# First segment's first Q, K and V products in full fp32 from the weights as loaded, in an attention and MLP kernel

## The chip, the core and the metric

The kernel runs on one core of a Trainium2 chip. The core has five engines that work from queues of their own and wait for one another by semaphores: TensorE (PE: matmuls, and PEld for its weight loads), VectorE (DVE), ScalarE (ACT), GpSimd (POOL) and SyncE (SP, which here only issues DMAs). Each engine takes its instructions strictly in the order in which the program issues them. The metric is the device time of one execution in microseconds (us).

## The reference

Two branches share a layer norm of `x` (2048 tokens, 512 features). Their outputs and `x` are added.

```python
xn = layernorm(x)
out = x + A(xn) + B(xn)

# A: 32 heads of 16, the tokens in 4 segments of 512
q, k, v = xn @ wq, xn @ wk, xn @ wv            # per head
for s in range(4):
    logits = q_s @ k_s.T / 4 + mask            # -1e9 where query < key
    a_dot = softmax(logits) @ v_s
    a_mem = (phi(q_s) @ M) / (phi(q_s) @ z + 1e-6)
    o_s = g * a_mem + (1 - g) * a_dot          # g = sigmoid(beta), per head
    M += phi(k_s).T @ v_s ;  z += sum(phi(k_s))
A = concat(o_s) @ wo                            # phi(t) = t + 1 if t > 0 else exp(t)
# B: MLP with 1792 hidden features
B = gelu(layernorm(xn) @ w1 + b1) @ w2 + b2
```

## The kernel before, in words

**Numbers in two halves.** Inputs are fp32. For most products the kernel splits a number into a high and a low fp16 part and computes three fp16 products (high-high, high-low, low-high), summed in PSUM (`split3`, L463). A product with 512 input features has 4 blocks of 128, and so 12 matmuls. Weights are scaled by a power of two ahead of the split, taken from the mean square of the weights. `w_square` (L286) sums the squares on ACT, `w_scale` and `qk_scale` (L336, L324) bring the sums over all partitions by a small matmul and compute the scales on DVE, and `w_split` (L366) splits one piece. A piece marked "V" in `SPLIT` is split by ACT (high part) and DVE (low part) out of the raw weights. One marked "G" is scaled in place by POOL, rounded by ACT and subtracted by POOL. The raw weights lie in the same tiles in which the halves are put, two pieces further on, or in staging tiles borrowed from `pt`, `oT` and others.

**Tokens.** The first four token tiles are loaded, normalised (`ln`, L432), transposed by PE and split into `xnT` (`ln_out`, `ln_tr`, L447 to L459: ACT writes the high half, DVE the low one, both from PSUM).

**Units.** A unit is one segment and eight of the 32 heads: 16 units, of which units 0 to 3 are the first segment. `qk_proj` (L477) computes Q or K of a unit for 512 tokens. ACT and DVE split the result into `hl`, of which there is a single buffer, and SP stores it to DRAM three times and loads it back as stacks `qst` or `kst`. For K (and for Q after the first segment) `phi` is computed too, and `pk_nat` (L502) transposes it. `v_nat` (L558) computes V of 128 tokens. `m_jobs` (L583) computes the logits and takes the masked maximum of each row on DVE (L601). `s_jobs` (L622) computes them again, transposed, and ACT takes the exponentials. `pv` (L657) multiplies with V in fp32, `o_norm` (L681) normalises, `out_jobs` (L779) applies `wo`. The MLP is in pieces as well: `d_jobs` (L717) is the hidden layer, `gelu` and `h_split` follow, and `e_part` (L758) is the second layer.

**The order of the work** is written out by hand as a string, `ORDER`: each letter names a stream (`streams`, L57), and the next job of that stream is issued. `BANKS` gives for each PSUM tile, in the order in which they are asked for, which of the eight banks it takes. Fourteen jobs of eight matmuls on constants (`warm_up`, L796) are strewn in.

Around the start the old order runs: loads of the tokens, of Q and K weights of the first head group ("qk"), of the other three ("QK"), of V; their squares on ACT among the norm and the transposes; the scales; then K of unit 0 (job 51 of 1307), the first V split, Q of unit 0 (67), the first hidden-layer product (68), K and Q of unit 1 (84, 99), and V of the four token blocks (88, 115, 118, 123). The first row maxima are jobs 92 to 95.

Of the kernel before, what the change touches and what calls it, by code (L numbers as in the profile page):

```python
# [19 lines left out]
P = 128  # L20
# [24 lines left out]
SPLIT = {"qk": "VV", "QK": "GVGVGV", "v": "VVVV", "1a": "GVGVGVG", "2a": "GVGVGVG", "1b": "GVGVGVG", "2b": "GVGVGVG",  # L45
# [11 lines left out]
def streams():  # L57
# [31 lines left out]
    for m in PARTS:  # L89
# [3 lines left out]
        if m == "v":  # L93
# [3 lines left out]
    zero = [("zero", 0), ("const",), ("zero", 1)]  # L97
    return [norm, again, wts, [("par2",)], zero, keys, queries, nat, maxi, soft, vals_p, heads, memo, vals, hid, act,
            mlp, outs, accs, [("warm", n) for n in range(14)]] + split
# [3 lines left out]
    "aacttcucccecuttauttvvvvaceaaccvueataccvctatbvwcwtcdfwvtuxxxhtyxxyxxgoyxswtxocwvxwyowfcxynoyziiiiyvzgoyiozczyozy"  # L103
    "pziiniznipiAnaciqizAzpooiimvBivhooAAiiqiqvpjpqjqqijqijziqiqwcjqqjiAsmzkBzkkkqjAiojssiqAjjoioBAjjaAfApooBgskkpkk"
    "jpjqlohoopjjljoojiiqilApkkkkjiqqiqAijqqjijqjjgpiiakkkkifpplqiiqqqqqqslooioppoiiioloosijiaaqaBsjqqjiqjijqiqjqiii"
    "paqkkmkkqiqajqqqjqjaaihbojjjgpBmkkkkBfoopjjloojjqljlooijqiBkpkkkijqipqiqjqqjiiqjjqqijqqiqmipikkkkmlignhillfpnrr"
    "mjjrjqjjnaiijpnsiiikkkkijoiijopojiqjiqijsrjikkkmkihlspomfoljjqqjqjmjgloojmkkmkkjqqjjqaqqjqjiqqjiqkkkmkippliiohf"
    "ooapliqqiqmqipgoopqqqiiiqqiqlsmoopoioppqiioojiqijqjqijooijjsoapamkkkkamjisithpqjisqjqjqaqjjaqqiiqqikkkkpiaalblo"
    "sfojqjqjqjqqjmjglkkmkmkjjoojjjomhojiipkkkkaiiipnplnpiliifnimigniilriarrmmsijjrjijoajqiiqjqiskkkksijqjqiqjqijqjq"
    "iqjiqipikkkkoilmhfoqpljjqjqmjgpjjpoooolmkmkkkohijsiqjqpiqijqiqjqqijiqqiqqiqjiqiipkkkkmoipllfmqqgoooopopopsjqjqj"  # L110
    "qjqqjqiiqpqiqiqipooqjiqiiqpilsmoooooaapikkskkpiqjaqjaaqjqqqqjijqjqaiamskkmkkblfoljmjhgjqqjqjqjqlomkkkkmjjjmooij"
    "iojiojiipkkkkpiifiinpiliinlnimlgmrjjjspnrojiqiqjqiqijqipkkkkqijqjsirjqijqjqijqiqiispkkkmkrpillfompgooopmjqjjooj"
    "mjqojsqiilkkkkpiqijqiqjqiqijjqijqiqjiqipsikkkkoilpolfojmjgpqjqjqqjjookkklmkpoiqjiqjqiqijqijopjjqiqiiqiqiqqipskk"
    "ppikoikplspoooqjqjljqqjqjjooolkpkpkkqqjqspmqqjjqqqqjqpqqjqqjmkkkkpmqqqlqqlqqqqlqqqrrrr"
# [5 lines left out]
    "012345670123546137402651372405614372051643720516437205164307265143027653027653062753062706532750362570376205376"  # L120
    "205376205362705326705326705326710452376104526371045263045320645036245063245063245063245063712450637124506372145"
    "061435601453601345601345601354607132547601325476013254670123546703456374056743065704365074356074630574630574630"
    "745630745630475162304753016247530164275031765420316750136017563017605310576310576035173650713650713657013657420"
    "136507421365021365021365021365021365021365210356210764235107462351074654213607326107326107326107326107613027613"
    "052743061527413056274153062741530627410532764105237641052376410523170562413760254103215043250143025143502145032"
    "145032145034215034276031524371605243716502654302643560423560423560423560423560427160427160427160427160427160427"
    "106427103564271035642710642710267410267410627410741674216704231560742031576402316574021365740213657402136574012"
    "365741230657412360531260523610523610352601365021635021635021635021635021632501637245016245062140562415061254065"
    "124065124065124065124056140256317405263174263172467321734621763241763241763417623417620345120342510342510342571"
    "60257"  # L130
# [17 lines left out]
def infini_mixer_kernel(ctx: ExitStack, tc: tile.TileContext, x, wq, wk, wv, wo, beta, w1, b1, w2, b2, out):  # L148
# [64 lines left out]
    qksc = cst.tile([P, 4, 2, NG], F32, name="qksc")  # L213
# [110 lines left out]
    def qk_scale(g0, n):  # L324
# [7 lines left out]
        V.tensor_scalar(qksc[:, 3, :, g0:g0 + n], s, float(2 ** 10), None, op0=OP.mult)  # L332
        V.tensor_tensor(qkcs[:, 0, g0:g0 + n], c[:, 0], c[:, 1], op=OP.mult)
        V.scalar_tensor_tensor(qkcs[:, 1, g0:g0 + n], f[:, 0], float(2 ** -16), f[:, 1], op0=OP.mult, op1=OP.mult)

    def w_scale(m):  # L336
# [18 lines left out]
        if m == "o":  # L355
# [27 lines left out]
    F1, S1, F2, S2, CG, SHH, C2, B1F = range(5, 21, 2)  # L383

# [76 lines left out]
    xnT = {}  # L461

# [14 lines left out]
    def qk_proj(i, which):  # L477
# [3 lines left out]
        split3(p, ((w, lambda w, k, a: w[:, g, a, P * k:P * k + P]),  # L481
                   (xnT[s], lambda t, k, a: t[:, k, a, :])), KT, True, True)
        phi = not (s == 0, s == NSEG - 1)[which]
        hl = sb.tile([P, 2, 512], F16, name="hl")
        A.activation(hl[:, 0, :], p, AF.Copy, scale=float(2 ** -16))
        if phi:
            e = sb.tile([P, 512], F32, name=("phq", "phk")[which])
            A.activation(e, p, AF.Exp, scale=qkcol(2, 1 - which, g))
# [8 lines left out]
        if phi:  # L497
            V.tensor_scalar(e, e, 1.0, qkcol(3, 1 - which, g), op0=OP.min, op1=OP.mult)
            V.scalar_tensor_tensor(e, p, 0.0, e, op0=OP.max, op1=OP.add)  # L499
            pqt[i, which] = e  # L500
# [383 lines left out]
```

## Time and profile before

| | |
|---|---|
| three runs, us | 708.18, 705.11, 708.0 (median 708.0) |
| profiled execution, us | 706.76 |
| its span, first to last instruction, us | 705.1 |
| granted TensorE clock over the span | 0.995 |
| instructions | 16658 |
| matmul records and their busy us | 6213, 683.4 |

The profile is one execution. Busy times are those of instructions at work on an engine; a PE that is busy is not at its peak for that, since the ends of its pipelined matmuls are modelled. A row of a group gives line, engine, operation, output and inputs, shape and count, then busy us and mean ns of one, then the engine's idle time just before them and what ended it. A row of the timeline gives the start, the busy time, and the instruction; several in a row of one kind are merged (x12). A row of the waits gives who waited for whom, the total, the times and the longest.

### The profile page before, as it was taken

The numbers are of one execution on the slowest core, as the hardware profiler recorded it, in microseconds if no ns is written. First come the engines' busy times: TensorE is split into PE (matmuls) and PEld (weight loads), VectorE is DVE, ScalarE is ACT, GpSimd is POOL, SyncE is SP. The second block draws the span as 40 slices with busy tenths as digits, with TensorE's granted clock in tenths as the row PEclk, the third lists the DMA queues.
The fourth block names the chain that finished last, engine by engine and source line by source line (L and its number), as shares of the span: only waits on it lengthen the run. The fifth ranks groups of instructions, "written<-read, shape, count | busy, mean of one in ns | idle before, by whom it ended". The sixth has DMA issues, their size and how long they took to land.

```text
span 705.1 us, 16658 instructions
## 1 busy us (share of the span) xinstructions
PE 683.4 (97%) x6213; PEld 395.6 (56%) x6213; DVE 545.1 (77%) x1734; ACT 517.8 (73%) x954; POOL 350.2 (50%) x532
## 2 busy tenths in 40 slices
PE   7779999999999999999999999999999999999997
PEld 6445656465644555567554456666554446555643
DVE  5599988798696867998689877969679676968533
ACT  6878888949786669568974597756686677887870
POOL 4265676463742435545454326355453445456652
PEclk9999999999999999999999999999999999999999
DMA  9966123141302322132222313141131313230001
GB/s 280 268 159 206 48 41 98 49 104 18 92 2 70 113 73 66 46 77 62 59 80 68 93 25 106 18 121 32 33 92 46 94 30 93 61 92 16 19 17 60
DMA packets 51791, 55.11 MB, mean 78 GB/s; under 512 B 4783, under 2 KB 40637, under 8 KB 51709
## 3 DMA queue, kind: packets, MB, share of 16 engines
q1 hardware_dynamic: 49404, 49.84, 25.0%
q0 software_dynamic: 2304, 4.20, 3.7%
q8 instruction: 49, 0.80, 0.5%
q14 instruction: 34, 0.27, 0.1%
HBM read 36.99 MB, written 17.04 MB: 77 GB/s over the span
## 4 chain that ended last, share of the span: by engine, by line
PE 74%; DVE 12%; ACT 8%; issue 2%; POOL 2%; DMA 1%; SPq 0%; POOLq 0%; DVEq 0%; ACTq 0%
PE ps L469 32%; PE ps L769 14%; PE ps L663 8%; PE ps L788 6%; PE ps L634 5%; PE ps L594 4%; DVE ps L601 4%; ACT pt L639 3%; PE ps L542 1%; ACT hT L736 1%; DVE mc L601 1%; DVE hT L729 1%; DMA pt<-in_A_wq_dram 1%; ACT hT L744 1%; PE ps L455 1%
## 5 line engine op out<-in xcount | busy, mean ns | idle before, releaser
L601 DVE CUSTOM_DVE_ANT_0 ps<-ps,mask 128x512 f32<-128x512 f32 (+3 forms) x512 | 234.1, 523 | 11.3 <-PE ps L594 10.0
L639 ACT ACTIVATE pt<-ps,qkcs 128x512 f32<-128x512 f32 (+1 forms) x384 | 205.4, 624 | 30.4 <-PE ps L634 25.5
L769 PE MATMUL ps<-w2s,hT 64*128 64x512 f16 x1344 | 175.9, 375 | 0.6 <-DVE fence L772 0.6
L469 PE MATMUL ps<-xnT,w1s 128*128 128x256 f16 x1344 | 159.0, 274 | 2.2 <-POOL w1s L378 0.8
L469 PEld LDWEIGHTS <-w1s 128*128 128x128 f16 x1344 | 129.1, 98 | 31.7 <-issue 11.5
L648 POOL TENSOR_SCALAR_AFFINE_SELECT pt<-pt 128x256 f32<-128x256 f32 x256 | 100.7, 422 | 80.8 <-ACT pt L639 80.1
L745 POOL TENSOR_TENSOR hT<-hh,hT 128x512 f16<-128x512 f32 x64 | 67.9, 1060 | 84.4 <-ACT hT L744 84.4
L769 PEld LDWEIGHTS <-hT 64*128 64x128 f16 x1344 | 74.3, 94 | 55.3 <-issue 8.1
L663 PE MATMUL ps<-pt,vt 128*32 128x256 f32 (+3 forms) x1024 | 77.7, 435 | 0.0
L601 DVE DVE_READ_ACCUMULATOR2_ANT mc<- 128x1 f32 x512 | 71.3, 139 | 0.1
L594 PE MATMUL ps<-kst,qst 48*128 48x512 f16 (+3 forms) x512 | 67.7, 297 | 1.9 <-DVE mc L601 0.7
L634 PE MATMUL ps<-qst,kst 50*128 50x512 f16 (+3 forms) x512 | 68.5, 297 | 1.0 <-DVE phk L499 0.6
L744 ACT ACTIVATE hT<-hh 128x512 f16<-128x512 f32 x64 | 36.7, 573 | 42.9 <-POOL hh L743 42.7
L729 DVE SCALAR_TENSOR_TENSOR hT<-ps,sc,sr 128x256 f32<-128x256 f32 x112 | 51.2, 477 | 21.7 <-PE ps L469 21.2
L663 PEld LDWEIGHTS ps<-pt,vt 128*32 128x32 f32 x1024 | 31.6, 109 | 40.9 <-issue 30.8
L743 POOL TENSOR_SCALAR hh<-hT,sc 128x512 f32<-128x512 f32 x64 | 42.2, 660 | 18.7 <-ACT hT L736 16.9
L736 ACT ACTIVATE hT<-hT,b1t 128x256 f32<-128x256 f32 x112 | 46.6, 496 | 4.0 <-DVE hT L729 3.8
L693 POOL TENSOR_TENSOR nN<-nN,oT 128x512 f32<-128x512 f32 x16 | 20.2, 1266 | 56.4 <-DVE oT L517 56.4
L469 PE MATMUL ps<-wvs,xnT 128*128 128x512 f16 x192 | 44.5, 382 | 3.6 <-DVE wvs L374 3.6
L634 PEld LDWEIGHTS <-kst 50*128 50x128 f16 x512 | 27.9, 94 | 30.6 <-issue 12.5
L469 PE MATMUL ps<-xnT,wqs 128*128 128x512 f16 x192 | 44.3, 380 | 0.6 <-DVE mc L601 0.6
L594 PEld LDWEIGHTS <-qst 48*128 48x128 f16 x512 | 28.2, 94 | 29.6 <-issue 13.3
(220 smaller groups left out, 931.7 us busy)
## 6 DMA issues: line engine op xcount, KB each, us to landing
kd<-hl SPq DMA_DIRECT2D x48, 128.0 KB
kst<-kd SPq DMA_DIRECT2D x32, 192.0 KB
qd<-hl SPq DMA_DIRECT2D x48, 128.0 KB
qst<-qd SPq DMA_DIRECT2D x32, 192.0 KB
acc<-in_A_x_dram SPq DMA_DIRECT2D x16, 256.0 KB
acc<-in_B_b_dram POOLq DMA_DIRECT2D x16, 256.0 KB, 4.2
out_dram<-acc SPq DMA_DIRECT2D x16, 256.0 KB
xt<-in_A_x_dram SPq DMA_DIRECT2D x14, 256.0 KB
```

What stands on the lines that cost most here:

```text
L469: T.matmul(p, wsl(ws, k, a), xsl(xs, k, b), start=s0 and i == 0, stop=s1 and i == 3 * n - 1)
L594: T.matmul(p[:, o:o + n], stk[i, 0][r, t, P * qb:P * qb + P], stk[i, 1][r, t, :n], start=True, stop=True)
L601: V.tensor_tensor_reduce(p[:, o:o + n], p[:, o:o + n], mask[:, 512 - n:], 1.0, -3e38, OP.add, OP.max, mc[i][:, 4 * b + t, qb:qb + 1])
L634: T.matmul(p[:, o:o + n], stk[i, 1][r, t, P * kb:P * kb + P], stk[i, 0][r, t, P * kb:], start=True, stop=True)
L639: A.activation(e[:, OFF[kbs[0]]:OFF[kbs[0]] + o], p[:, :o], AF.Exp, scale=qkcs[:, 1, i % NG:i % NG + 1])
L648: G.affine_select(v, v, pattern=[[0, 2], [1, P]], compare_op=OP.is_ge, fill=0.0, base=0, channel_multiplier=-1)
L663: T.matmul(p[32 * c:32 * c + 32, P * kb:], vt[s, kb][:, 4 * g + c, 16 * odd:16 * odd + 32], pt[i, 2 * c + odd][:, OFF[kb]:OFF[kb] + LEN[kb ...
L729: V.scalar_tensor_tensor(hz[:, fi, :], p[:, :256], col(CG + fh), srow[hs][:, own], op0=OP.mult, op1=OP.mult)
L736: A.activation(z, z, AF.Gelu_apprx_tanh, bias=b1t[:, FH * (j % 2) + f:FH * (j % 2) + f + 1])
L744: A.activation(hT[:, z, 0, :], t, AF.Copy)
L745: G.tensor_tensor(hT[:, z, 1, :], t, hT[:, z, 0, :], op=OP.subtract)
L769: T.matmul(pes[j][a], hTs[fh][r, fi, u, P * a:P * a + P], w2s[r, fo, v, :], start=n == 0 and m == 0, stop=fi == FH - 1 and m == 2, skip_gr ...
```

## The change

For the first segment Q and K of units 0 and 1 and V of all four token blocks are computed in full fp32 from raw weights and fp32 tokens: four matmuls of 512 columns in place of twelve in fp16. For that `first_tr` builds four fp32 tiles, each with the 512 tokens of 128 features (transposed by PE, copied out of PSUM by ACT or DVE in turns, in tiles borrowed from `oT`, `rt` and `phq`). `first_split` makes the fp16 halves of `xnT` for the first segment out of them, now from SBUF. The scales that the split path has in its weights are applied when results leave PSUM. The second piece of K is split by ACT and DVE instead of POOL, so that the raw weights of both second pieces last. All other products, of the first segment too, stay as they were, and so all weights are still split.

```diff
-SPLIT = {"qk": "VV", "QK": "GVGVGV", ...
+SPLIT = {"qk": "VV", "QK": "VVGVGV", ...
...
+    first = [("Xs", k) for k in range(KT)]
...
-    qksc = cst.tile([P, 4, 2, NG], F32, name="qksc")
+    qksc = cst.tile([P, 5, 2, NG], F32, name="qksc")
...
+        V.tensor_scalar(qksc[:, 4, :, g0:g0 + n], s, float(2 ** -6), None, op0=OP.mult)
...
-        if m == "o":
+        if m == "v":
+            V.tensor_scalar(col(SV0), col(SV), float(2 ** -6), None, op0=OP.mult)
+        elif m == "o":
...
+        if n == 0:
+            return first_tr(2 * b + k)
...
+    def first_tr(k):
+        p = dense()
+        for j in range(4):
+            T.transpose(p[:, P * j:P * j + P], lt[0, j // 2][j % 2][:, P * k:P * k + P], ident)
+        if k < 2:
+            t = sb.tile([P, 2, 512], F16, name="oT", bufs=4).rearrange("p a c -> p (a c)").bitcast(F32)
+        else:
+            t = sb.tile([P, 512], F32, name=("rt", "phq")[k - 2])
+        if k % 2:
+            V.tensor_copy(t, p)
+        else:
+            A.activation(t, p, AF.Copy)
+        x32[k] = t
+
+    def first_split(k):
+        h = xnT[0][:, k, 0, :]
+        A.activation(h, x32[k], AF.Copy, scale=1024.0)
+        V.scalar_tensor_tensor(xnT[0][:, k, 1, :], x32[k], 1024.0, h, op0=OP.mult, op1=OP.subtract)
...
+        raw = i < 2
+        if raw:
+            r = piece("qk"[which], g)
+            for k in range(KT):
+                T.matmul(p, r[:, P * k:P * k + P], x32[k], start=k == 0, stop=k == KT - 1)
+        else:
+            split3(...)
...
+        f = qkcol(4, 1 - which, g) if raw else float(2 ** -16)
+        A.activation(hl[:, 0, :], p, AF.Copy, scale=f)
...
-        A.activation(pkn[i], p.rearrange("p (a b) -> p a b", a=4), AF.Copy)
+        A.activation(pkn[i], p.rearrange("p (a b) -> p a b", a=4), AF.Copy, scale=qkcol(3, 0, i) if i < 2 else 1.0)
...
+        if s == 0:
+            for k in range(KT):
+                T.matmul(p, x32[k][:, P * b:P * b + P], piece("v", k), start=k == 0, stop=k == KT - 1)
+        else:
+            split3(...)
...
-                     scale=float(2 ** -16))
+                     scale=col(SV0) if s == 0 else float(2 ** -16))
```

`ORDER` and `BANKS` are new from the first letters to the last (1311 jobs, of which four are `first_split`, and as many PSUM tiles as before). The start of the new order: the two norm applications and all eight squares of Q and K weights come ahead of the four `first_tr` jobs (28, 30 to 32). Then, among others, the first x split (35), both V squares (37, 38), the scales of "QK" (40), the second x split (41), Q of unit 0 (45), the other x splits (47, 48), the "qk" splits (49, 50), two w1 squares (53, 54), K of unit 0 (55), V of blocks 0 and 1 (59, 60), Q of unit 1 (73), V of block 2 (74), the first two hidden-layer products (75, 78), the first row maxima (81, 82), K of unit 1 (86) and V of block 3 (94). The loads keep their sequence, except that those of w2 (second part of the first half) and of w1's second half are issued after the stores of Q of unit 0, and later K of unit 0, which stand on the same SP queue. From about job 200 on the same jobs have been issued in both orders, but for the four x splits and a handful of weight jobs: two splits of w2 and the squares of `wo` come later in the new one.

More of the change, by code (lines that the diff above doesn't have):

```diff
@@ L97, in streams @@
     zero = [("zero", 0), ("const",), ("zero", 1)]
+    first = [("Xs", k) for k in range(KT)]
     return [norm, again, wts, [("par2",)], zero, keys, queries, nat, maxi, soft, vals_p, heads, memo, vals, hid, act,
-            mlp, outs, accs, [("warm", n) for n in range(14)]] + split
+            mlp, outs, accs, [("warm", n) for n in range(14)]] + split + [first]
 ORDER = (
-    "aacttcucccecuttauttvvvvaceaaccvueataccvctatbvwcwtcdfwvtuxxxhtyxxyxxgoyxswtxocwvxwyowfcxynoyziiiiyvzgoyiozczyozy"
-    "pziiniznipiAnaciqizAzpooiimvBivhooAAiiqiqvpjpqjqqijqijziqiqwcjqqjiAsmzkBzkkkqjAiojssiqAjjoioBAjjaAfApooBgskkpkk"
@@ L105 @@
[L105 to L109, printed above, removed]
@@ L131 @@
+    "562370562370562370253625706325710463527014635216341562341653241563215632156321546315247630147630147630147630154"
+    "27015"
 )
```

58 lines of the change are left out of this document (32 added, 26 removed).

## The prediction

> **What bounds the kernel now.** I read the page's busy shares first, then the table of stretches, then the chain of waits at the start, and then the timeline of the first 60 us. The profiled execution took 706.8 us for a span of 705.1; 1.7 us lie around the span. The median of the runs shown is 708.0, so my sum, made against 706.8, stands 1.2 us under that median. About 0.5% (3.5 us: below 703.2 or above 710.3) is what a measurement of this kernel can tell from no change.
>
> ```profile
> PE 683.4 (97%) x6213; PEld 395.6 (56%) x6213; DVE 545.1 (77%) x1734; ACT 517.8 (73%) x954; POOL 350.2 (50%) x532
> ```
>
> The columns of the stretches are: bounds, length, busy us (count) of PE, PEld, DVE, ACT, POOL, the granted clock, DMA share, GB/s.
>
> ```profile
> 0.00:20.00 20.00, 15.87 (x113) 11.89 (x114) 12.29 (x47) 13.59 (x31) 9.30 (x23) 1.00 1.02 281
> 20.00:40.00 20.00, 15.63 (x100) 10.54 (x99) 12.81 (x48) 16.13 (x26) 8.02 (x9) 0.91 0.81 240
> 40.00:60.00 20.00, 15.94 (x100) 9.00 (x99) 18.95 (x46) 14.69 (x27) 11.81 (x11) 0.91 0.65 184
> 60.00:80.00 20.00, 19.08 (x164) 10.78 (x163) 19.62 (x79) 16.56 (x32) 12.39 (x13) 1.00 0.45 136
> 80.00:100.00 20.00, 18.76 (x219) 12.38 (x215) 18.21 (x73) 17.56 (x36) 14.43 (x24) 1.00 0.21 34
> 100.00:690.00 590.00, 586.98 (x5476) 336.45 (x5476) 458.82 (x1442) 438.60 (x805) 291.97 (x454) 1.00 0.24 62
> ```
>
> There are two kernels in one. From 100 us on PE is busy for 587.0 of 590 us. Before that PE is not the bound: it is idle for 14.7 of 100 us, and most of the warm-up matmuls (16.3 us in all, a row further down) are filler too. From 40 to 95 us the full engine is DVE (18.95, 19.62 and 18.21 of 20), with row maxima, weight splits and scalings. In the first 40 us nobody is full, and DVE loses time that it lacks later. So the early stage is DVE's load up to about 95 us plus what DVE waits before that, and from there on the end is a fixed amount of PE work away. DVE's waits in the first 100 us (total, times, longest):
>
> ```profile
> DVE w1s L374 <- ACT w1s L373: 2.9, 1, 2.9
> DVE st L395 <- DMA xt<-in_A_x_dram: 2.5, 1, 2.5
> DVE hT L729 <- PE ps L469: 2.4, 3, 1.0
> DVE hl L489 <- ACT phk L488: 1.7, 1, 1.7
> DVE nw L404 <- ACT nw L403: 1.6, 1, 1.6
> DVE fa L347 <- PE ps L345: 1.4, 1, 1.4
> DVE xnT L459 <- ACT xnT L458: 1.2, 1, 1.2
> DVE wks L284 <- PEq L870: 0.9, 1, 0.9
> DVE wks L374 <- ACT wks L373: 0.5, 1, 0.5
> DVE hl L489 <- ACT hl L485: 0.2, 1, 0.2
> ```
>
> They come to 15.3 us. The change can win only here: through fewer waits, through less DVE work ahead of 95 us, or by leaving PE less to do from there.
>
> **The products themselves.** Eight products change: Q and K of units 0 and 1, and V of the four token blocks. Each has 12 fp16 matmuls of 512 columns now and gets four fp32 ones.
>
> ```profile
> L663 PE MATMUL ps<-pt,vt 128*32 128x512 f32 x256 | 34.9, 603 | 0.0
> L594 PE MATMUL ps<-kst,qst 48*128 48x512 f16 x128 | 27.7, 378 | 0.2
> ...
> L594 PE MATMUL ps<-kst,qst 48*128 48x128 f16 x128 | 16.8, 214 | 0.0
> L801 PE MATMUL ps<-ones 128*128 128x256 f16 x112 | 16.3, 303 | 1.6 <-POOL ones L171 1.6
> ...
> L663 PE MATMUL ps<-pt,vt 128*32 128x128 f32 x256 | 13.8, 273 | 0.0
> ```
>
> Mean times hold a fixed latency that a stream hides, so I take slopes. An fp16 record costs (378 - 214) / 384 = 0.427 ns per column. An fp32 record costs (603 - 273) / 384 = 0.859 ns, and one fp32 matmul leaves two records: L663 issues 512 of them (16 units, 2 halves, 4 blocks, 4 tiles) and the four forms hold 1024 records. A product now streams for 12 x 512 x 0.427 = 2.62 us, and in fp32 for 8 x 512 x 0.859 = 3.52 us: +0.90 us each, **+7.2 us of PE work**. I cost it at nothing, since all eight lie ahead of 95 us, where PE has 14.7 us idle and most of 16.3 us of filler. Without that cover it costs 7.2 us less the earlier start below.
>
> **The start.** K of unit 0 starts at 18.30 now, because it needs split tiles of x and split weights.
>
> ```profile
> 13.51 0.57 ACT L458 ACTIVATE xnT<-ps 128x512 f16<-128x512 f32 x1
> 13.98 0.62 ACT L310 ACTIVATE wks<-pt 128x512 bf16<-128x512 f32 x1
> ...
> 17.73 1.06 ACT L310 ACTIVATE wvs<-wvs 128x1024 bf16<-128x1024 f32 x1
> ...
> 18.30 2.76 PE L469 MATMUL ps<-xnT,wks 128*128 128x512 f16 x12
> ...
> 20.86 7.34 SPq L276 DMA_DIRECT2D w1s<-in_B_w_dram  x4
> ...
> 23.77 1.70 ACT L310 ACTIVATE w1s<-w1s 128x1792 bf16<-128x1792 f32 x1 [0.37 <-DMA w1s<-in_B_w_dram]
> ...
> 50.11 0.69 DVE L601 CUSTOM_DVE_ANT_0 ps<-ps,mask 128x512 f32<-128x512 f32 x1
> ```
>
> Afterwards Q of unit 0 comes first and needs four fp32 tiles. The new order puts all eight squares of the Q and K weights ahead of ACT's first copy, where six stand now, so that copy moves from 13.51 to about 13.5 + 2 x 0.62 = 14.8. Two ACT copies of about 0.57 follow, and the first product starts at about 16.0, **2.3 us earlier** than 18.30.
>
> On SP's queue three stores and two loads of Q of unit 0 now pass in front of the second load of w2 (2a) and of all loads of w1's second half. These loads hold SP for 7.34 us from 20.86, with the first stores of K behind them. Moving the stores ahead costs nothing as long as the loads are in by about 33 us (w2) and 48 us (w1), where their squares stand in ACT's new queue. The squares of w1's first half still cannot start before 23.77: those loads keep their place.
>
> **DVE's waits after the change**, from the new order and these rows. The first 0.9 and 2.5 stay: 3.4. The wait in the normalisation (1.6) loses one square of 0.62 that stood ahead of its two activations: 1.0. The two waits at the transposed tiles and the first split (1.7) become about 2.2: ACT's copies are 1.3 later, and DVE's own two copies fill part of it. The two at hl (1.9) stay near 2.0, with other causes: the split of the second x tile and the hl of Q stand behind both V squares (1.06 each), and K's hl stands behind two w1 squares that start at 23.77 with 1.70 each. The wait of the V scale for PE (1.4) goes: its squares are done early. The split of w1 (2.9) becomes about 2.4, for the hl of Q of unit 1, which stands behind a w2 square of like length. Of the three at L729 one goes (1.0), which came from V waiting for its split weights: 1.4. The sum is 3.4 + 1.0 + 2.2 + 2.0 + 0 + 2.4 + 1.4 = 12.4, against 15.3: **-2.9 us**.
>
> **DVE's work ahead of 95 us.** Two of the four transposes are now copied by DVE before they are split.
>
> ```profile
> L729 DVE SCALAR_TENSOR_TENSOR hT<-ps,sc,sr 128x256 f32<-128x256 f32 x14 | 6.5, 474 | 2.4 <-PE ps L469 2.4
> ...
> L459 DVE SCALAR_TENSOR_TENSOR xnT<-ps,xnT 128x512 f16<-128x512 f32 x4 | 2.7, 687 | 1.3 <-ACT xnT L458 1.2
> ```
>
> The trace has no such copy; 0.47 (L729, half the length) and 0.69 (L459, the full length and one input more) bound it, and I take 0.6, nearer to the row of its length: 1.2 in all. One split of K goes from POOL to DVE.
>
> ```profile
> L374 DVE SCALAR_TENSOR_TENSOR w1s<-w1s,sc x5: 751/1460/1639, 34.0 to 72.2; 128x512 f16<-128x512 f32 x5
> ```
>
> That is 0.75 at the least and 1.64 at the most. I take 0.75, since this split comes near 20 us, when POOL has little to do. The three added scale columns are tiny instructions, 0.5 with their gaps. Together **+2.45 us**. The other way goes one DVE split of w2, which the new order puts behind the point that PE reaches at 95 us: **-0.75**. The split of x reads the same amount as now, and ACT's two copies (0.57 each) lie in the queue counted above. Two weight splits that used POOL's in-place scaling must now keep the raw weights, which is the same edit. The end of the order differs in where the last head's two steps stand between e parts; PE's queue there is the same, so I cost it at nothing. The rest of the order and the banks are new, too; a stretch with 587 of 590 us busy leaves them little to win, and perhaps 2 us to lose or win by chance.
>
> **The sum:** -2.9 + 2.45 - 0.75 = -1.2, so 706.8 - 1.2 = **705.6 us**: no change that can be told.
>
> **Rivals.**
>
> *Faster: DVE is fed early.* If ACT gets through its squares in time and V's splits, no longer urgent, meet a quiet POOL, the waits of 2.2, 2.0 and 2.4 shrink. All of them gone gives 705.6 - 6.6 = 699.0; half gives 702.3, which is this rival's time. For it: DVE's first row maximum comes at 50.11 although K and Q of unit 0 are done well before, so there is room. Against it: ACT was already busy 16.13 of 20 us from 20 to 40 us, and it gets two copies more.
>
> *Slower: PE becomes the early bound.* Six fp32 products (21.1 us) stand ahead of the first hidden-layer product in PE's queue, which can't come before 16.0 + 21.1 = 37 us. If the GELU, the e parts and DVE's row maxima then wait on PE, the 7.2 us are paid in full less the 2.3 of the earlier start: 706.8 + 4.9 = 711.7. It decides as soon as PE has no idle time or filler left between 37 and 95 us. Against it: PE idles 6.2 us between 40 and 100 by the stretches above, and V's products were only moved from there, not added.
>
> *Slower within the band: the two-input splits collide with POOL.* The split of x reads PSUM and SBUF now; afterwards it reads two SBUF tiles, like L374, whose row runs from 0.75 to 1.64 for one shape. If all four go from 0.69 to 1.46, that row's median, they cost 3.1 us: 708.7. Against it: POOL has little to do near 20 us. The Trainium skill states the rule for this, in "GPSIMD Engine Reference", Specifications: GpSimd's SBUF interfaces are shared with VectorE, with contention for VectorE instructions that have two SBUF inputs. By that rule this case would need POOL to be busy during the splits; the spread of L374 in this trace agrees with it.
>
> **How the numbers follow.** The forecast has 0.36, the collision 0.10; both lie within 0.5%, with small parts beyond it on either side that offset each other. Faster has 0.35, the early PE bound 0.19. So faster 0.35, same 0.46, slower 0.19. The range takes in the full removal of the waits below (699.0) and the paid PE work above (711.7), and no more than the chance of the new order's remainder lies outside: 699 to 712.
>
> **What would show it.** The first fp32 product near 16 us with four matmuls (eight records) in about 3.5 us. DVE's waits ahead of 100 us near 12 us. First row maximum on DVE near 45 us but behind the same load, so that the first e parts and the first exponentials come within 3 us of now, and a busy PE from about 95 us. The prediction is wrong if PE is full from 60 us on (early bound), if DVE's waits fall under 8 us (fed early), or if the span from 100 to 690 us changes its PE work by over 3 us, which would be the new order and not the products.

## The result, and the profile after

| | before | after |
|---|---|---|
| median of the runs, us | 707.64 (705.11 to 708.18) | 714.82 (714.27 to 718.45) |
| ratio, 95% interval | | 1.0122 [1.0105, 1.0139] |
| profiled execution, us | 706.76 | 714.51 |
| its span, us | 705.1 | 712.8 |
| granted clock | 0.995 | 0.995 |

The change costs 7.2 us by the medians and 8.6 by the ratio. 705.6 was forecast, with a range of 699 to 712: the time lies outside it, on the slow side. (A single run of all that follow, one of new_start_free_bank_200 at 2457 us, was disturbed and is left out of its median.)

The busy shares of the changed kernel, and its table of stretches (the same columns as before: bounds, length, busy us and count of PE, PEld, DVE, ACT, POOL, the granted clock, DMA share, GB/s):

```profile
PE 695.2 (98%) x6181; PEld 397.9 (56%) x6181; DVE 551.1 (77%) x1740; ACT 520.0 (73%) x957; POOL 347.3 (49%) x530
```

```profile
0.00:20.00 20.00, 17.41 (x95) 12.00 (x96) 13.89 (x45) 13.98 (x33) 10.06 (x23) 1.00 0.92 293
20.00:40.00 20.00, 20.00 (x78) 10.53 (x76) 17.76 (x50) 19.02 (x32) 6.20 (x7) 1.00 0.77 230
40.00:60.00 20.00, 20.00 (x136) 12.58 (x134) 19.12 (x68) 15.55 (x29) 12.16 (x13) 1.00 0.51 136
60.00:80.00 20.00, 16.30 (x179) 8.74 (x177) 18.36 (x70) 13.20 (x22) 13.05 (x17) 0.91 0.51 169
80.00:100.00 20.00, 19.66 (x182) 11.19 (x179) 16.93 (x69) 18.18 (x39) 11.60 (x21) 1.00 0.11 23
100.00:690.00 590.00, 583.32 (x5407) 334.72 (x5407) 455.82 (x1428) 437.52 (x804) 289.01 (x449) 1.00 0.24 63
```

PE has no idle time from 20 to 60 us now, and DVE is busier there than it was. But from 60 to 80 PE starves for 3.7 us, 2.6 of them waiting for DVE's row maxima, and the clock falls to 0.91: PE had run ahead of DVE. Behind 100 us the row that the forecast rested on has changed. PE is busy for 583.3 of 590 us instead of 587.0, so it idles 6.7 us in the place of 3.0.

The products themselves, in the timeline of PE (start, busy us, engine, line, operation):

```profile
14.63 1.88 PE L514 MATMUL ps<-oT,wqs 128*128 128x512 f32 x4
16.35 1.02 PE L514 MATMUL ps<-rt,wqs 128*128 128x512 f32 x2
17.21 1.02 PE L514 MATMUL ps<-phq,wqs 128*128 128x512 f32 x2
...
22.08 1.88 PE L598 MATMUL ps<-wvs,oT 128*128 128x512 f32 x4
23.80 1.02 PE L598 MATMUL ps<-pt,rt 128*128 128x512 f32 x2
24.66 1.02 PE L598 MATMUL ps<-pt,phq 128*128 128x512 f32 x2
25.52 1.02 PE L598 MATMUL ps<-wvs,oT 128*128 128x512 f32 x2
```

Q of unit 0 starts at 14.63 (18.30 was the first product before). One product takes 25.52 - 22.08 = 3.44 us.

**Where the time is lost: lag at equal work.** Two different orders can't be compared job by job. So I give each PE record the steady time of its form, read off its longest gapless runs (a matmul of the hidden layer 0.108 us, by two rows shown further down; a product counts the same in both forms, and filler counts nothing). I add these up along the time and ask how much later a kernel reaches the same sum than the kernel before does. The number at 700 us is close to the difference of the spans (7.6 against 7.7). It is worked out from all PE rows of both timelines. In the table of all profiles further down the entry at 700 us misses the difference of the spans by up to 1.4 us, so a single entry is good to about 1 us.

```
us                    40     60    100    160    340    700
after               -8.3  -12.3   -1.8    0.6    4.1    7.6
```

PE is 12 us ahead at 60 us, gives 10.5 of it back by 100 us, and from there loses 9.4 us. So in this execution the start ended where the forecast had it (-1.2 forecast, -1.8 here), and the loss lies in the long stretch behind it, where none of the products stands.

### The profile page after: what moved, and what is told of

Read it like the earlier page. It is cut to its first block, busy times and chain, and to the rows that moved or that the text cites. A ratio compares the mean times of both kernels' runs of the same rounds, so it can differ in the third digit from the quotient of the medians.

```text
span 712.8 us, 16634 instructions
## 1 busy us (share of the span) xinstructions
PE 695.2 (98%) x6181; PEld 397.9 (56%) x6181; DVE 551.1 (77%) x1740; ACT 520.0 (73%) x957; POOL 347.3 (49%) x530
## 4 chain that ended last, share of the span: by engine, by line
PE 67%; ACT 13%; DVE 11%; POOL 3%; issue 3%; DMA 3%; POOLq 0%; SPq 0%; DVEq 0%; ACTq 0%
PE ps L498 24%; PE ps L809 15%; PE ps L703 8%; PE ps L634 4%; ACT pt L679 4%; PE ps L674 4%; PE ps L828 4%; DVE ps L641 2%; PE ps L514 2%; PE ps L598 2%; PE ps L578 1%; ACT hT L776 1%; POOL hT L785 1%; ACT hT L784 1%; DMA qd<-hl 1%
## 5 line engine op out<-in xcount | busy, mean ns | idle before, releaser
L703 PE MATMUL ps<-pt,vt 128*32 128x512 f32 (+3 forms) x1024 | 77.6, 436 | 0.1
L674 PE MATMUL ps<-qst,kst 50*128 50x512 f16 (+3 forms) x512 | 70.1, 298 | 3.4 <-DVE mc L641 1.6
L634 PE MATMUL ps<-kst,qst 48*128 48x256 f16 (+3 forms) x512 | 68.0, 298 | 3.4 <-DVE mc L641 1.8
L733 POOL TENSOR_TENSOR nN<-nN,oT 128x512 f32<-128x512 f32 x16 | 20.8, 1300 | 51.2 <-DVE oT L553 51.2
L828 PE MATMUL ps<-wos,oT 128*128 128x512 f16 x192 | 43.3, 379 | 0.1
L498 PE MATMUL ps<-xnT,wqs 128*128 128x512 f16 x168 | 40.3, 392 | 0.0
```

The lines of the kernel that those rows point to most:

```text
L498: T.matmul(p, wsl(ws, k, a), xsl(xs, k, b), start=s0 and i == 0, stop=s1 and i == 3 * n - 1)
L634: T.matmul(p[:, o:o + n], stk[i, 0][r, t, P * qb:P * qb + P], stk[i, 1][r, t, :n], start=True, stop=True)
L674: T.matmul(p[:, o:o + n], stk[i, 1][r, t, P * kb:P * kb + P], stk[i, 0][r, t, P * kb:], start=True, stop=True)
L703: T.matmul(p[32 * c:32 * c + 32, P * kb:], vt[s, kb][:, 4 * g + c, 16 * odd:16 * odd + 32], pt[i, 2 * c + odd][:, OFF[kb]:OFF[kb] + LEN[kb ...
L828: T.matmul(p, o[:, u, P * b:P * b + P], wos[:, g, v, :], start=i == 0, stop=i == 3 * NG - 1)
```

## The experiments

Two theories stood at the outset. **A**: the products' PE work is covered, and the loss is the new order of the rest. **B**: the 8 x 0.9 us of fp32 work are paid after all, and the loss behind 100 us is that work in disguise. The second rival, that the products or the copies cost something where they stand, was tried alone too. The time of the kernel before stood at 706.9 to 707.2 us beside these runs. The lags of all profiles are in one table behind the experiments.

### The two orders spliced

```diff
 ORDER, new_start_old_rest (and _260: cut at 260)
   jobs 1 to 200 of the new order (first_tr, fp32 products)
-  jobs 201 to 1311 of the new order and its banks
+  the jobs that are left, in the old order and with the old banks
 ORDER, old_start_new_rest
+  jobs 1 to 200 of the old order, no fp32 products
   the jobs that are left, in the new order
 ORDER, products_in_old_order
+  the old order; x splits behind their transposes; V splits 2, 3 behind V of block 3
```

> The first 200 jobs of the new order (fp32 products, x splits and all), then all other jobs in the old order with the old kernel's bank pattern. Theory A, the re-planned rest is what costs: the two traces have the same PE work done 1.8 us earlier with the change at 100 us, and 7.6 us later at the end, so the loss of some 9 us lies behind job 200 and goes: 703 to 706 us, 0.3 to 0.6% under before. Theory B, the fp32 products' 7 us of PE work are paid at the end: they are all still there, so 712 to 715 us.

> As the first kernel, but with the first 260 jobs in the new order. Theory A: 703 to 706 us, and within 2 us of the first kernel, as the loss lies spread over the stretch from 100 us on; if it is much slower, part of the loss lies between jobs 200 and 260. Theory B: 712 to 715 us.

> The kernel before with its own first 200 jobs and no fp32 product, then all other jobs in the new order with the new bank pattern. Theory A (the rest costs): 714 to 718 us, as slow as the change or slower, since the small gain at the start is not there. Theory B (the products cost): 706 to 708 us, as before.

> The eight fp32 products, the fp32 tiles and the x splits in the old order with the old banks; only the last two V splits are moved behind V of block 3, since raw V weights lie where they write. Theory A: PE has idle time and filler for the products, so 705 to 709 us. Theory B: 7 us of PE work on top, 712 to 714 us.

| | us, median (lowest to highest) | ratio, 95% |
|---|---|---|
| new_start_old_rest | 718.08 (716.73 to 718.72) | 1.0152 [1.0136, 1.0167] |
| new_start_old_rest_260 | 717.59 (715.48 to 717.79) | 1.0140 [1.0124, 1.0157] |
| old_start_new_rest | 719.82 (718.98 to 721.65) | 1.0183 [1.0166, 1.0199] |
| products_in_old_order | 712.59 (710.94 to 712.83) | 1.0068 [1.0054, 1.0083] |

(In this and all later kernels with the new start ahead of the old rest, one warm-up that the new order has at 152 us stands beside those at the start.)

By their medians the kernels with the new start ahead of the old rest miss what theory A expected of them and lie above theory B's times too: the splice costs by itself. `products_in_old_order` missed theory A's range as well and stands where theory B had it (712 to 714). At the seam a weight's squares or scale, whose load had been planned elsewhere, stand in the queue ahead of it. But where the time goes tells the theories apart. `old_start_new_rest` has none of the products and loses 10.7 us between 100 and 700 us. `new_start_old_rest` loses all it loses by 120 us and nothing from there on. `products_in_old_order` has all the products and loses 4.5 us in the first 100 us, and nothing behind (its span is 4.2 us longer).

### Mending single waits of the new order

Behind 100 us the waits of PE in the changed kernel, largest first (total, times, longest):

```profile
PE ps L498 <- DVE nD L717: 1.7, 1, 1.7
PE ps L674 <- DVE mc L641: 1.4, 1, 1.4
PE ps L634 <- DMA qst<-qd: 1.0, 1, 1.0
PE ps L578 <- DVE zr L567: 0.9, 2, 0.5
```

The kernel before has none over 0.6 there. One place looked worst, in the timeline of the changed kernel:

```profile
351.03 1.26 POOL L733 TENSOR_TENSOR nN<-nN,oT 128x512 f32<-128x512 f32 x1
351.11 2.96 DVE L567 TENSOR_TENSOR zr<-bd,mst 64x64 f32<-64x64 f32 x4
...
352.37 1.26 POOL L735 TENSOR_TENSOR nN<-nN,ame 128x512 f32<-128x512 f32 x1
...
352.65 1.09 PE L578 MATMUL ps<-phq,zr 64*128 64x512 f32 x2 [0.40 <-DVE zr L567]
...
354.21 1.09 PE L578 MATMUL ps<-phq,zr 64*128 64x512 f32 x2 [0.47 <-DVE zr L567]
...
355.24 4.45 PE L498 MATMUL ps<-xnT,wqs 128*128 128x512 f16 x12
```

```profile
352.00:356.00 4.00, 3.13 (x11) 0.91 (x8) 2.20 (x5) 3.37 (x7) 3.92 (x7) 0.93 0.73 165
356.00:360.00 4.00, 4.00 (x16) 1.69 (x15) 1.33 (x2) 0.66 (x2) 1.69 (x4) 0.65 0.38 62
```

The row sums of unit 7 (job Z(7): four DVE instructions that lay out `M` and `z` for the matmul of job Qd(7), L578) stand three jobs ahead of their use (54 in the old order), beside two POOL instructions that read two SBUF tiles each. They take 2.96 us, PE waits twice, the granted clock falls to 0.65 in the next 4 us, and a product that takes 2.76 us at full clock takes 4.45.

```diff
 ORDER, z7_early
+ Z(7) S(7,0,0) ...
  ... A(7,0) O(6,2)
- Z(7)
  S(7,2,2) A(7,1) Qd(7) T(8,0)
 ORDER, four_moves: also
+ both late warm-ups (152 and 332 us) beside the sixth; M(3,1), e(2,0), e(2,1) ahead of S(2,0,0);
+ e(13,0), e(13,1) ahead of M(15,0)
 ORDER, five_moves: also
+ ws(o,1), ws(o,2), ws(o,3) behind N(4)
```

> The changed kernel with one job, the repeated row sums of unit 7 on VectorE, moved 13 jobs earlier, ahead of S of unit 7's first block; nothing else. Theory A (the loss against the kernel before, 7.2 us by the medians, is made of single waits that the new order of the rest puts into the PE-bound part): the wait at 352 to 356 us and the low clock of 356 to 360 us go, which the lag at equal work puts at 3 to 5 us, so 710 to 712 us and a ratio of 1.004 to 1.008. Theory B (the loss is the PE work of the eight fp32 products, 8 x 0.9 us): nothing changes, 713 to 716 us. A third case, that the wait only moves to another job: 713 to 715 us with the lag rising by the same 4 us elsewhere.

> The five moves without the one of the wo splits, behind which PE waited 3.1 us at about 190 us. If that wait was the whole harm of the five moves: 712 to 714 us. If the other four waits were worth what their rows say (1.0, 1.0, 3.9 and 1.3 us) and nothing takes their place: 708 to 711 us. Theory C (waits come back elsewhere): 714 to 716 us, as the changed kernel.

> The changed kernel with five moves in its order: the two late warm-up jobs (at 152 and 332 us) put beside the warm-up at the start; the row sums of unit 7 earlier as in the run beside this one; the three later splits of wo moved behind N(4); M(3,1), e(2,0) and e(2,1) ahead of S(2,0,0); e(13,0) and e(13,1) ahead of M(15,0), for which M(15,0), M(15,1) and S(14,1,1) take other banks. Theory A (single waits of the new order): the waits are worth 1.0 + 1.0 (warm-up), 3.9 (row sums), 2.0 (wo splits), 1.9 and 1.3 us, 11 in all, of which some come back elsewhere: 704 to 708 us, ratio 0.995 to 1.001. Theory B (the products' PE work is paid): 713 to 716 us.

z7_early: 715.49 us (714.41 to 716.20), 1.0124 [1.0103, 1.0145]. four_moves: 714.79 (712.27 to 716.15), 1.0107 [1.0089, 1.0125]. five_moves: 718.62 (716.11 to 720.84), 1.0164 [1.0138, 1.0189]. The changed kernel had 1.0122. So none of them is told from it but five_moves, which is slower. The 710 to 712 us that theory A expected of z7_early and the 704 to 708 of five_moves were missed; four_moves came out as theory C had it (the waits come back elsewhere). In the stretches of z7_early the place itself is mended:

```profile
352.00:356.00 4.00, 3.94 (x34) 1.61 (x34) 2.68 (x6) 3.50 (x7) 2.22 (x4) 1.00 0.43 120
356.00:360.00 4.00, 4.00 (x28) 2.28 (x30) 0.74 (x1) 2.85 (x6) 4.00 (x8) 1.00 0.41 83
```

From 340 to 360 us this execution loses 0.9 us instead of 3.7, near the 3 to 5 us that theory A put on the place. But at 80 us it stood 2.5 us further back than the changed kernel's profile did (lags of 0.1 and -2.4), with the same jobs up to there, and that takes up nearly all of the gain. The other moves did not even mend their own places: from 140 to 160 us four_moves loses 2.5 us, the changed kernel 2.1, though a warm-up of 1.0 us and a wait of 1.4 us were taken away (new waits of 0.8, 0.4 and 0.6 us came). And the moved splits of five_moves opened a new wait, larger than any that was there, as the timelines of PE and DVE show:

```profile
203.17 0.40 PE L634 MATMUL ps<-kst,qst 48*128 48x384 f16 x4 [3.14 <-DVE ame L584]
```

```profile
198.39 0.83 DVE L378 SCALAR_TENSOR_TENSOR wos<-wos,sc 128x512 f16<-128x512 f32 x1 [1.60 <-ACT wos L377]
200.01 1.12 DVE L378 SCALAR_TENSOR_TENSOR wos<-ame,sc,wos 128x512 f16<-128x512 f32 x1 [0.79 <-ACT wos L377]
...
202.38 1.53 DVE L584 TENSOR_SCALAR ame<-ps,bg 64x512 f32<-64x512 f32 x2
```

The scaling of unit 4's product with `M` (L584), which frees the banks that PE's next logits need, now stands behind two splits that wait for ACT. So theory A in its simple form falls: the loss is not a handful of waits that can be taken out one by one.

### Mending the seams

```diff
 ORDER, new_start_mended_215 and _260: new order for 215 or 260 jobs, then the old one
+  squares of wo behind M(2,8), H(2,1), e(1,13); scale of wo ahead of ws(o,0)
 ORDER, new_start_free_bank_200 and _215
+  as these, but the scale of wo ahead of D(3,1), in a bank read long before
```

> The new order for its first 215 jobs with the fp32 products, and behind them the order and banks of the kernel before, with the squares and the scale of wo put later so that none of them stands ahead of its load at the seam. Theory A (the products and the start win about 2 us, the new rest loses about 9): the lag against the kernel before is -3 to +1 us at 120 us and stays flat behind it, 704 to 708 us. Theory B (the products' work is paid behind 100 us): the lag rises by 5 to 7 us between 100 and 700 us, 712 to 715 us. If the seam stalls again, the lag jumps once between 90 and 140 us and is flat behind that.

> As the run beside it, with the new order for its first 260 jobs. Theory A: 704 to 708 us, lag flat behind 140 us. Theory B: 712 to 715 us, lag rising to 700 us. If the two seams differ by more than 3 us, the difference is the seam's and not the order's.

> The new order with the fp32 products for its first 200 jobs and the old order and banks behind them, with the loads, squares and the scale of wo put later, the scale ahead of D(3,1) and in a bank that has long been read. Theory A (the new rest loses 6 to 9 us behind 100 us and the old rest nothing; the single jump of the mended seams was the scale of wo waiting for its bank): the lag at equal work is -2 to +1 us at 100 us and the same within 1.5 us at 700 us, 704 to 708 us. Theory B (any order with the products pays their 7.2 us of PE work behind 100 us): 712 to 715 us with a lag that rises all the way. Theory C (each change of a planned order opens a wait where there was none, so that a seam always costs some us): a lag that jumps once by 3 us or more within 60 us of the seam and is flat behind it, 710 to 715 us.

> As the run beside it, cut at 215 jobs: against the mended seam at 215 jobs (713.84 us) only the scale of wo moves, ahead of D(3,1) and into a free bank. There PE waited 2.5 us for that bank at 158 us and 1.8 us at 163 us. Theory A: both waits go, 4.3 us less, 708 to 710 us, lag flat behind 165 us. Theory C: the waits come back at other lines, 712 to 714 us.

| | us, median (lowest to highest) | ratio, 95% |
|---|---|---|
| new_start_mended_215 | 713.84 (711.09 to 717.02) | 1.0101 [1.0074, 1.0128] |
| new_start_mended_260 | 719.49 (716.39 to 721.82) | 1.0171 [1.0147, 1.0195] |
| new_start_free_bank_200 | 716.94 (712.20 to 718.93) | 1.0130 [1.0103, 1.0158] |
| new_start_free_bank_215 | 714.06 (710.45 to 715.12) | 1.0088 [1.0067, 1.0109] |

None reaches 708 us by its median. The seam of new_start_mended_215 stalls once more, for a new reason, as the timeline of PE shows:

```profile
147.55 2.78 PE L498 MATMUL ps<-xnT,w1s 128*128 128x256 f16 x24
...
151.38 4.09 PE L498 MATMUL ps<-xnT,w1s 128*128 128x256 f16 x36
...
160.48 0.39 PE L345 MATMUL ps<-am,ones 128*128 128x3 f32 x2 [2.46 <-DVE xnT L466]
...
164.47 0.27 PE L634 MATMUL ps<-kst,qst 48*128 48x256 f16 x1 [1.77 <-ACT pt L679]
```

(The first two rows give the steady time above: (4.09 - 2.78) / 12 = 0.109 us.) The scale of wo took a bank that DVE had not yet read. In a free bank it waits for a row maximum (1.9 us) and the next products for its own column (1.3 us) instead. That is theory C of the expectations: every place that a planned order did not foresee costs some us, and the cost is paid once. Behind 160 us all these kernels are flat or gain. (The profile of new_start_free_bank_200, further down, is that of an execution of 712.20 us, the shortest that it had.)

### The products' work, and the copies, alone

The two half_products kernels leave out two of the four blocks of each of the eight products, so their output is not that of the reference.

```diff
 half_products (new order), half_products_in_old_order
-            for k in range(KT):
+            for k in (0, KT - 1):
                 T.matmul(p, r[:, P * k:P * k + P], x32[k], start=k == 0, stop=k == KT - 1)
 (the same in v_nat)
 copies_alone_in_old_order: the old order, all eight products by split3
-        raw = i < 2
+        raw = False
 (the same in v_nat, old scales; first_tr, first_split and the three scale columns stay)
```

> The changed kernel whose eight fp32 products each sum over two of the four groups of 128 rows only (half of each product is left out, 8 x 1.72 = 13.8 us of PE work less). If the products' PE work is paid in the end (theory B): 701 to 706 us. If it is covered, since VectorE and ScalarE set the time where the products stand, and the loss is the rest of the order's (theory A): 711 to 715 us, with PE's work in the first 60 us shorter by 13.8 us, more waiting there, and the same lag growing behind 160 us by 3.5 to 7.5 us.

> The products in the old order (712.59 us, 4.8 us above the kernel before by the profiles' lag), each over two of the four groups only (half left out, 13.8 us of PE work less). Theory B: 704 to 708 us. Theory A with VectorE's extra work and waits as the cost of the start: 710 to 713 us.

> The old order and the old three-term products, with the copies of the first segment's transposed tiles and the splits of x out of the copies (all of the change's extra work on VectorE and ScalarE for x, none of its products, and no V split moved). If VectorE's extra work is paid one for one where it is bound: 2.0 to 3.5 us above the kernel before, 709 to 710.5 us. If the copies are hidden: 706.5 to 707.5 us. If the later splits of x hold up the first products (copy, then split, in a row on two engines): 710 to 713 us, as products_in_old_order.

| | us, median (lowest to highest) | ratio, 95% |
|---|---|---|
| half_products | 717.58 (716.19 to 719.29) | 1.0152 [1.0131, 1.0173] |
| half_products_in_old_order | 708.93 (707.22 to 711.00) | 1.0031 [1.0018, 1.0044] |
| copies_alone_in_old_order | 709.45 (708.18 to 710.25) | 1.0033 [1.0021, 1.0044] |

Two rows of the changed kernel, then the same two of half_products:

```profile
0.00:60.00 60.00, 57.41 (x303) 35.11 (x305) 50.78 (x161) 48.54 (x91) 28.41 (x42) 1.00 0.73 220
60.00:100.00 40.00, 35.96 (x357) 19.93 (x354) 35.29 (x138) 31.38 (x60) 24.65 (x37) 0.96 0.31 96
```

```profile
0.00:60.00 60.00, 45.98 (x245) 29.22 (x246) 46.71 (x147) 46.27 (x87) 27.30 (x41) 0.89 0.74 220
60.00:100.00 40.00, 35.73 (x361) 19.73 (x360) 35.65 (x143) 31.50 (x59) 23.25 (x33) 0.96 0.31 95
```

PE has 11.4 us less to do in the first 60 us, in spite of a granted clock of 0.89, and the kernel is not faster but 3 us slower than the changed one (slower than the 711 to 715 us that theory A had, while theory B had 701 to 706). In the new order none of the products' work is paid: theory B falls. In the old order the same cut brings 712.59 down to 708.93. That is 3.7 us for 13.8 us of work, or 0.27 us each, so the 7.2 us that fp32 adds are worth some 1.9 there. The copies, splits and scale columns alone cost 0.33% (0.21 to 0.44%), 2.3 us, which is what DVE's extra work was put at (2.45). DVE's waits ahead of 100 us come to 15.3 us in that kernel, as in the kernel before, so it is the work and not waiting.

### All profiles side by side

Lag at equal work against the kernel before, in us, each of one execution, and PE's idle time in the 530 us from 160 to 690 us (530 less the busy time in the row of that stretch). The half products are set off by the 10.4 us of work that they leave out by this count (half of 8 x 12 x 0.216 us); of half products the last column is at 680 us.

```
                                 100    160    340    700   idle 160:690
rest in the old order
  before                           -      -      -      -       2.6
  copies_alone_in_old_order      1.9    1.8    2.3    1.2       2.4
  half_products_in_old_order     1.5    1.4    0.5    0.4       2.4
  products_in_old_order          4.5    4.2    4.4    2.8       3.4
  products_earlier_in_old_order 11.6   11.7   11.4   10.6       2.5
  new_start_old_rest             9.6   11.6   12.3   11.3       3.5
  new_start_old_rest_260        -0.3    8.4    9.0    7.7       3.4
  new_start_mended_215           0.2    6.9    6.8    5.2       4.4
  new_start_mended_260           3.3   13.4   14.6   13.0       7.1
  new_start_free_bank_200        3.4    6.3    5.6    4.2       2.1
  new_start_free_bank_215        4.4    8.2    8.7    7.4       3.3
rest in the new order
  after                         -1.8    0.6    4.1    7.6       4.6
  z7_early                       0.7    3.5    6.0    7.0       4.6
  four_moves                     0.8    3.9    6.8    8.4       4.6
  five_moves                     0.1    2.3    8.8    9.8       6.9
  half_products                  1.8    4.5    9.8   11.8       5.2
  old_start_new_rest             1.1    5.9    8.8   11.8       4.9
```

Three of the rows from which the last column comes, the kernel before, the changed one, and old_start_new_rest, which has none of the products:

```profile
160.00:690.00 530.00, 527.43 (x4937) 299.97 (x4934) 407.24 (x1280) 392.37 (x719) 255.14 (x401) 1.00 0.23 60
```

```profile
160.00:690.00 530.00, 525.39 (x4848) 299.15 (x4846) 408.75 (x1293) 390.13 (x716) 253.87 (x401) 1.00 0.23 60
```

```profile
160.00:690.00 530.00, 525.10 (x4838) 298.95 (x4836) 408.83 (x1304) 389.77 (x714) 253.85 (x397) 1.00 0.24 61
```

From 160 us to 700 the ten kernels with the old rest gain 0.3 to 2.1 us. The six with the new rest lose 3.5 to 7.5, with the products, with half of them and without them. (With the difference of the spans in place of the column at 700 us it is from 1.4 us gained to 0.3 lost for the ten, and 4.1 to 8.0 lost for the six.) From 100 to 160 us the new order takes another 2.2 to 3.1 (4.8 behind the old start, whose seam lies there). That separation of the lags holds in every profile, and it is what I call shown. Order and banks were always changed together, so it is the two in one that lose; which of them does was not tried. (The idle time separates them too, but for the two mended seams, whose stall reaches past 160 us.)

The last kernel of the table moved Q's product of unit 0 up in the old order:

```diff
 ORDER, products_earlier_in_old_order
  T(0,1)
+ T(0,0)
  scale of wv ... N(0) ... scale of w1 ...
- T(0,0)
```

> The products in the old order (712.59 us), with the Q product of unit 0 moved right behind the K product, ahead of the scales of wv and w1 and of their waits. If the 5 us that the products cost there come from their place at the start (PE waits 2.2 us for the scales' column with the Q product queued behind it): the lag at 40 us falls from 5.2 to 2 to 3 us and the time to 709 to 711 us. If they come from VectorE's extra work (2.5 us) and from the products' PE work: no change, 711 to 713 us.

719.21 us (717.18 to 720.64), 1.0177 [1.0160, 1.0195]: 6.6 us worse than products_in_old_order, where 2 to 4 better had been expected. The wait went, and one of 6.6 us for the squares of w1's first half came (first row), against 2.2 us for the scales' column before (second row, products_in_old_order). ACT had got Q's first half of `hl` ahead of those squares. It waits 5.65 us until K's half has been stored out of the single buffer `hl` (third row, ACT's timeline), and the squares behind it hold up every hidden-layer product:

```profile
PE ps L345 <- ACT w1s L311: 6.6, 1, 6.6
```

```profile
PE ps L541 <- DVE fa L349: 2.2, 1, 2.2
```

```profile
32.40 0.69 ACT L521 ACTIVATE hl<-ps,qksc 128x512 f16<-128x512 f32 x1 [5.65 <-DMA kd<-hl]
```

## Why the prediction was wrong, step by step

**The first product, 2.3 us earlier:** right in kind, short in size. It came at 14.63, 3.7 us earlier: ACT's first copy of a transposed tile started at 13.78, not at 14.8. One product took 3.44 us (3.52).

**DVE's waits, 15.3 to 12.4:** near. The waits of DVE ahead of 100 us in the changed kernel come to 11.2 us. These are the largest:

```profile
DVE st L400 <- DMA xt<-in_A_x_dram: 3.0, 2, 2.4
DVE hT L769 <- PE ps L498: 1.3, 1, 1.3
DVE w1s L378 <- ACT w1s L377: 1.2, 1, 1.2
...
DVE hl L525 <- ACT phk L524: 1.1, 1, 1.1
```

**DVE's extra work, +2.45:** right in the sum; the copies, splits and columns alone cost 2.3 us. Of its terms the two copies took 0.68 us each (0.6), and K's split 1.09 (0.75). The 0.75 us taken off for a split of w2 had no ground: in the profile before that split starts at 96.54 us, behind the 95 us to which the sum counts.

**The products' PE work at nothing:** right in the new order, as half_products shows. In the old order about a quarter of it would have been paid.

**The sum of the start, -1.2 us:** -1.8 in the profiled execution, but this was luck. In the eight profiles of kernels that have the new order for at least 215 jobs and all of its products the lag at 100 us goes from -1.8 to +4.4, with a mean of 0.9. The same jobs (after and z7_early) stood 2.5 us apart at 80 us, where PE, having run ahead of DVE, starves and its clock falls at different moments (0.63 from 76 to 80 us in the one, 0.61 from 64 to 68 us in the other). So the start won about nothing, and its outcome scattered.

**The step that failed** is this one: "The rest of the order and the banks are new, too; a stretch with 587 of 590 us busy leaves them little to win, and perhaps 2 us to lose or win by chance." Little to win was right. The loss was mis-sized: 9.4 us in the profiled execution, 6.3 to 10.7 in the others with the new rest. In a stretch that idles 3 of 590 us a different order can win 3 us at most. What it can lose isn't bounded by the idle time that was there, and for the 2 us the prediction gave no row. I had the evidence at hand: 54 jobs of lead for Z(7) in the old order against three in the new one were to be read off the order strings. The profile was predicted to show "if the span from 100 to 690 us changes its PE work by over 3 us, which would be the new order and not the products"; it changed by 3.7.

**The rivals.** DVE fed early (702.3): the first row maximum on DVE and the first exponential on ACT came at

```profile
41.65 0.69 DVE L641 CUSTOM_DVE_ANT_0 ps<-ps,mask 128x512 f32<-128x512 f32 x1
```

```profile
73.62 1.26 ACT L679 ACTIVATE pt<-ps,qkcs 128x512 f32<-128x512 f32 x2
```

instead of 50.11 and 80.50 us. The waits that this rival named (2.2, 2.0 and 2.4 in the forecast) came to 0.4, 1.4 and 1.2 us, so its condition was met by about half, as it asked. But other waits came in their place, 1.2 us of the row maxima for PE among them, and the lead was gone by 100 us. PE as the early bound (711.7): its time is nearest to what was measured, by chance. Its condition, no idle time and no filler of PE between 37 and 95 us, did not come true: PE is full from 20 to 60 us, but with warm-ups among its work from 50 us on, and from 60 to 80 it idles 3.7 us. And half the products' work gone brings nothing. The collision with POOL (708.7) did not come where it was looked for: the four splits of x took 0.68 to 0.69 us each. One of them ran beside a POOL instruction all the same. Then POOL's took longer (1.23 us; most of its kind take 0.69), and so did K's split behind it, in the timeline of the changed kernel:

```profile
18.56 1.23 POOL L380 TENSOR_SCALAR pt<-pt,qksc 128x512 f32<-128x512 f32 x1 [0.93 <-DVE qksc L332]
...
18.62 0.68 DVE L490 SCALAR_TENSOR_TENSOR xnT<-oT,xnT 128x512 f16<-128x512 f32 x1
...
19.22 1.09 DVE L378 SCALAR_TENSOR_TENSOR wks<-wks,qksc 128x512 f16<-128x512 f32 x1
```

**What stays open.** Why the new rest loses at places that no single row explains. Of the 9.4 us, PE's longer idle time from 100 to 690 us makes up 3.7, the low clock around 356 us 1.7 (0.07 and 0.35 of 4 us, by the rows of 352 to 360 us), and one late warm-up more than the old order has 1.0. The other 3 us do not show in the busy times. By place, 3.7 lie between 340 and 360 us, of which 2.8 were gone in the one profile with Z(7) moved. The remainder is spread over 100 to 220 and 500 to 640 us, and moving what waited there moved the wait. An order that joins the new start to an unharmed rest was not found: the five seams at 100 us or later cost 2.9 to 10.1 us between 100 and 160 us. No version beat the kernel before.

## What to carry to other kernels

When a change comes with a re-planned order, treat the order as a change of its own and as the larger risk: in a stretch where the bounding engine idles half a percent, a new order has next to nothing to win and several us to lose. Compare how far ahead of its consumer each short step of another engine stands in both orders. An engine that is let run ahead of the one that sets the pace only meets its wait later; here 12 us of lead at 60 us were 1.8 at 100 us, and nothing in the mean of eight profiles. To find out whether added work is paid, leave half of it out: the answer (no, in the one order; a quarter, in the other) did not depend on any seam.

## What the runs showed of the hardware

Four small DVE instructions with two SBUF inputs took 2.96 us beside two POOL instructions of 1.26 us each (L567, L733 and L735, above). Away from these they were short: in z7_early, beside two POOL instructions of 0.47 us, they took 1.13 us, and the same four for the next unit, with POOL at rest, 0.72 us. The rows of that line give the least, the middle and the longest time in ns, first between 330 and 360 us in the changed kernel, then in z7_early, then between 370 and 380 us in the changed kernel:

```profile
L567 DVE TENSOR_TENSOR zr<-bd,mst x4: 208/804/1260, 351.1 to 353.6; 64x64 f32<-64x64 f32 x4
```

```profile
L567 DVE TENSOR_TENSOR zr<-bd,mst x4: 207/320/424, 351.8 to 352.5; 64x64 f32<-64x64 f32 x4
```

```profile
L567 DVE TENSOR_TENSOR zr<-bd,mst x4: 214/216/222, 374.4 to 374.9; 64x64 f32<-64x64 f32 x4
```

The Trainium skill has the rule in "GPSIMD Engine Reference", Specifications: GpSimd shares its SBUF interfaces with VectorE, with contention for VectorE instructions that have two SBUF inputs. The trace agrees here, in a place that the forecast did not look at. At the splits of x, where it did look, DVE lost nothing: there it was POOL's instruction that took longer (1.23 us).

Two waits of PE of 0.40 and 0.47 us within 2 us were followed by 4 us at a granted clock of 0.65. The Trainium skill ("TensorE: Matmul & The Clock Gate", What's actually happening) has the clock fall after an idle window of about 3.4 us. PE did not idle for that long in this place: it was busy for 3.13 of the 4 us before. So the measured clock decides here, and an estimate of a short wait by its row alone is too low: the waits of 0.87 us and the 1.7 us that the low clock took make up most of the 2.8 us that z7_early lost less in this place.
